# A gated decode step: the output product in 16 whole and 16 halved row groups, with TensorE's end in a third code block

## The chip, the cores and the metric

The kernel runs on one core of one Trainium2 chip. A time is the device time of one execution in microseconds. A core has five engines that run their own programs and meet at semaphores: TensorE (matmuls), VectorE, ScalarE, GpSimd, and SyncE, which here issues all transfers from memory.

## What is computed

Four sequences decode one token each. One branch is attention over the last 4096 positions of a key and value cache (32 query heads on 8 key/value heads), the other is a gated feed-forward layer on the same token; a scalar gate per sequence mixes them.

```python
W = min(4096, max(256, Sk // 4))                       # 4096
q = (x @ wq) -> [4, 32, 1, 128]
k, v = the last W positions of k_cache, v_cache, each kv head for 4 query heads
p = softmax(q @ k.T * 128 ** -0.5)
a = (p @ v) -> [4, 4096] @ wo                           # wo: 4096 x 512
gate, up = x @ W_gate, x @ W_up                        # 512 x 1792 each
b = (gate * (gate > 0) * up) @ W_down                  # 1792 x 512
g = sigmoid((x * gate_w).sum(-1, keepdims=True))
return g * a + (1 - g) * b
```

x is 4 x 1 x 512, all arrays are bf16.

## The kernel before

The caches are worked through in eight sets (`NSET`), each one sequence and four of its eight kv heads: 4 MB of keys and 4 MB of values. All loads go through SyncE's single queue in the order that `_dma_order` writes out: wq, x, the gate weights, then keys and values in turn, W_gate and W_up, the last values, W_down, and wo in pieces. Memory on the core has four big slots; the values of all sets use the same one, so the values of a set wait until the value product (PV) of the set before is done (`_slots`).

A set s goes through these steps, in the order that `_order` writes out. VectorE transposes the keys in four parts (EKT), TensorE multiplies each part with the queries (SC, eight matmuls), VectorE masks and takes maxima (ESC), a small matmul spreads the maximum (SW), ScalarE takes the exponential (EXP), VectorE transposes the probabilities (EPT), and TensorE multiplies them with the values (PV, 32 matmuls: 16 on the first half of the slot, 16 on the second). ScalarE, for the last set also VectorE, copies the result to `osb` (NORM).

After the last set's scores TensorE computes gate and up (GU) and the sums of the softmax (RS), then PV of the last set. RELU on ScalarE and H on VectorE make the hidden row, EHT transposes and gates it. OQ (8 matmuls) and EOQ arrange the attention output into `oq`; FFN (14 matmuls) multiplies the hidden row by W_down, and WO multiplies `oq` by wo, both into the same accumulator. FIN copies the result, half on ScalarE and half on VectorE, and SyncE sends it out.

WO has 32 row groups i of 128 rows each. A group is either one whole matmul of 512 columns, or two half products of 256 columns that go to different columns of the array and different output rows (0 to 3 and 64 to 67); FIN reads the one half of the result from the first rows and the other from the second. `WHOLE` says how many groups are whole. `WO_PIECES` cuts wo into pieces in units of half a group (64 units of 64 KB); each piece is one transfer with a semaphore of its own, and the first matmul of a piece waits for it.

TensorE's program is not unrolled over the sets. It is cut into blocks (setup, turn, gates, half, first, value, mix, tail) with branches between them, and the semaphores are counted down as they are taken (`E.take`) so that the same code serves each set. At its start it marks a place, `here`, and a branch at its end, whose condition is never true, is announced there with `branch_hint(here)`. The other engines' programs have such an announced branch at their ends too, and GpSimd, ScalarE and SyncE place theirs at an aligned address with `addr_align`.

## Time and profile before

| | |
|---|---|
| median of the runs shown | 195.67 us (195.67, 195.49, 196.94) |
| the profiled execution's own time | 197.35 us |
| its span, first to last instruction | 194.6 us |
| data moved | 81.01 MB, 416 GB/s over the span |
| mean granted TensorE clock | 0.877 of full speed |
| matmuls in WO | 27 of 512 columns, 10 of 256 columns |

The span is the time from the first to the last of the program's own instructions; the execution's own time has 2.75 us more around it. PE is TensorE's matmuls, PEld its weight loads, DVE VectorE, ACT ScalarE, POOL GpSimd, SP SyncE; a q behind a name is that engine's sequencer. In rows of the timeline the first number is the start, the second the duration, and brackets hold the idle time before and what ended it. In the table of windows each engine has its busy time with the number of instructions, then follow the granted clock, the share of the transfer engines and GB/s. In the table of transfers the last number is the median time from issue to landing.

### The profile page before, as it was taken

The numbers are of one execution on the slowest core, as the hardware profiler recorded it, in microseconds if no ns is written. First come the engines' busy times: TensorE is split into PE (matmuls) and PEld (weight loads), VectorE is DVE, ScalarE is ACT, GpSimd is POOL, SyncE is SP. The second block draws the span as 40 slices with busy tenths as digits, with TensorE's granted clock in tenths as the row PEclk, the third lists the DMA queues.
The fourth block names the chain that finished last, engine by engine and source line by source line (L and its number), as shares of the span: only waits on it lengthen the run. The fifth ranks groups of instructions, "written<-read, shape, count | busy, mean of one in ns | idle before, by whom it ended". The sixth has DMA issues, their size and how long they took to land. (4 is left out here: it accounts for less than half of the span.)

```text
span 194.6 us, 1787 instructions
## 1 busy us (share of the span) xinstructions
PE 122.3 (63%) x651; PEld 56.4 (29%) x651; DVE 126.1 (65%) x156; ACT 30.5 (16%) x51; POOL 18.8 (10%) x42
## 2 busy tenths in 40 slices
PE   0025078489576927692779285928692879645896
PEld 0011022135122402340234022402340234222584
DVE  5114779999699459935993599359935993280300
ACT  2000000042220340034003400340034003400100
POOL 5984000100100010001000100010001000100000
PEclk9999558999969985999589969985999589997999
DMA  6999999999999999999999999999999989999991
GB/s 216 431 439 431 431 438 431 438 445 445 408 421 445 431 431 438 431 445 431 431 431 431 431 438 438 431 431 431 431 431 445 431 377 427 435 424 424 418 417 76
DMA packets 3906, 81.01 MB, mean 416 GB/s; under 512 B 441, under 2 KB 450, under 8 KB 834
## 3 DMA queue, kind: packets, MB, share of 16 engines
q1 hardware_dynamic: 3906, 81.01, 97.4%
HBM read 81.01 MB, written 0.00 MB: 416 GB/s over the span
## 5 line engine op out<-in xcount | busy, mean ns | idle before, releaser
L342 PE MATMUL bank<-kt,qblk 128*128 128x512 bf16 x256 | 73.6, 447 | 30.4 <-PEq L84 30.4
L560 DVE STREAM_TRANSPOSE kt<-slots 128x2048 f32<-128x2048 f32 x32 | 73.0, 2299 | 5.4 <-DMA slots<-in_A_k_cache_dram 5.4
L342 PEld LDWEIGHTS bank<-kt,qblk 128*128 128x128 bf16 x256 | 26.8, 110 | 73.5 <-issue 56.1
L342 PE MATMUL bank<-slots,pT 128*64 128x512 bf16 x256 | 31.0, 395 | 15.5 <-PEq L84 15.5
L598 DVE CUSTOM_DVE_ANT_0 sc<-bank,maskf 128x512 bf16<-128x512 f32 x32 | 21.5, 670 | 26.5 <-PE bank L342 26.5
L342 PEld LDWEIGHTS bank<-slots,pT 128*64 128x64 bf16 x256 | 17.4, 113 | 28.4 <-issue 20.6
L674 ACT ACTIVATE osb<-bank 32x256 bf16<-32x256 f32 x30 | 11.3, 375 | 89.2 <-PE bank L342 89.0
L688 ACT ACTIVATE pe<-sc,negmax 128x2048 bf16<-128x2048 bf16 x8 | 16.0, 2002 | 46.2 <-DVE negmax L608 46.2
L613 DVE STREAM_TRANSPOSE pT<-pe 128x2048 bf16<-128x2048 bf16 x8 | 18.3, 2285 | 2.2 <-ACT pe L688 2.2
L329 POOL COPY qblk<-qblk 128x576 bf16<-128x576 bf16 x8 | 5.3, 668 | 144.4 <-PE bank L342 144.4
L346 PE MATMUL bank<-identb,xsb 5*128 5x5 bf16 x4 | 0.3, 173 | 13.1 <-DMA xsb<-in_A_x_dram 13.1
L342 PE MATMUL bank<-rd,grpb 128*128 128x32 bf16 x8 | 1.4, 176 | 9.5 <-PEq L84 9.5
L342 PE MATMUL bank<-slots,oq 128*68 128x512 bf16 (+1 forms) x37 | 6.6, 350 | 0.0
L651 DVE CAST xsb<-bank 4x256 bf16<-4x256 f32 x1 | 0.4, 418 | 8.9 <-PE bank L342 8.9
L342 PEld LDWEIGHTS bank<-slots,oq 128*68 128x68 bf16 (+1 forms) x37 | 5.6, 164 | 1.0 <-issue 0.3
L342 PE MATMUL bank<-slots,xT 128*8 128x512 bf16 (+1 forms) x64 | 5.2, 486 | 0.6 <-DVE negmax L608 0.4
L564 DVE COPY xT<-bank 128x16 bf16<-128x16 bf16 x1 | 0.2, 166 | 7.7 <-PE bank L346 7.7
L622 DVE CAST osb<-bank 32x256 bf16<-32x256 f32 x2 | 0.8, 424 | 6.6 <-PE bank L342 6.6
L342 PEld LDWEIGHTS bank<-rd,grpb 128*128 128x128 bf16 x8 | 0.8, 96 | 13.2 <-issue 13.2
L346 PEld LDWEIGHTS bank<-identb,xsb 5*128 5x128 bf16 x4 | 0.2, 114 | 13.1 <-DMA xsb<-in_A_x_dram 13.1
L318 POOL MEMSET oq<- 128x4096 bf16 x1 | 3.5, 3512 | 0.1
L297 POOL TENSOR_SCALAR_AFFINE_SELECT fold<-fold 128x256 bf16<-128x256 bf16 x8 | 3.3, 418 | 1.1
(51 smaller groups left out, 39.1 us busy)
## 6 DMA issues: line engine op xcount, KB each, us to landing
slots<-in_A_k_cache_dram SPq DMA_DIRECT2D x8, 4096.0 KB, 24.8
slots<-in_A_v_cache_dram SPq DMA_DIRECT2D x6, 4096.0 KB, 15.6
slots<-in_A_v_cache_dram SPq DMA_DIRECT2D x4, 2048.0 KB, 12.6
slots<-in_A_wq_dram SPq DMA_DIRECT2D x1, 4096.0 KB, 12.3
slots<-in_B_W_gate_dram SPq DMA_DIRECT2D x1, 1792.0 KB, 19.3
slots<-in_B_W_up_dram SPq DMA_DIRECT2D x1, 1792.0 KB, 23.0
slots<-in_B_W_down_dram SPq DMA_DIRECT2D x1, 1792.0 KB, 17.6
slots<-in_A_wo_dram SPq DMA_DIRECT2D x1, 1408.0 KB, 19.7
```

Source lines behind the costliest of these rows:

```text
L297: op(lambda: e.affine_select(dst, src, pattern, cmp, fill, base=base, channel_multiplier=mult), ev)
L318: op(lambda: e.memset(oq[:, :, :], 0.0), ("PADQ",))
L329: E.op(lambda s=s: e.tensor_copy(qblk[:, 0, :, :, :], qblk[:, (s + 1) % NSET, :, :, :]), ev=("QC", s), ctr="qc", waits=[("SC", s, 3)])
L342: E.op(lambda: t.matmul(out_, lhsT, rhs, start=start, stop=stop, tile_position=pos, skip_group_check=True), ev=ev, waits=waits)
L346: E.op(lambda: t.transpose(out_, in_, idn), ev=ev, waits=waits)
L560: E.op(lambda: v.transpose(kt[:, f % 2, :].bitcast(FP32), slot("k", s)[:, 4096 * f:4096 * f + 4096].bitcast(FP32)), ev=("E", "KT", s, f), ...
L598: E.op(lambda: v.tensor_tensor_reduce(sc[:, 512 * f:512 * f + 512], banks[scb(key)], R["maskf"][:, :], 1.0, -3.0e38, ALU.add, ALU.max, mx4 ...
L613: E.op(lambda: v.transpose(pT[:, :], pe[:, :]), ev=("E", "PT", s), ctr="pt", waits=[("EXP", s)] + ([("PV", s - 1)] if s else []) + ([("V", ...
L622: norm(E, lambda d, p: v.tensor_copy(d, p), s, ((0, 1), (1, 1)), "NORMV")
L651: E.op(lambda: v.tensor_copy(osum[:, 256:512], banks[ACX][64:68, 256:512]), ev=("OSUM", 1), waits=[("WO", "P")])
L674: norm(E, lambda d, p: a.activation(d, p, ACTF.Copy), s, parts[0:2 if s == NSET - 1 else 4], "NORM")
L688: E.op(lambda: a.activation(pe[:, :], sc[:, :], ACTF.Exp, bias=negmax[:, s % 2:s % 2 + 1], scale=SCALE, accum_out=rowsum[:, s:s + 1]), ev= ...
```

## The change

`WHOLE` goes from 27 to 16, and wo comes in four pieces instead of five. The first half of the last values waits for the first half of the product of set 6 (`PVH`) instead of all of it; the second half waits for all of it. VectorE does the last EPT behind H instead of ahead of it. In TensorE's program the branch out of `mix` becomes the one that is announced at the program's start; in `tail` a second place is marked, and the never-taken branch at the end is announced there. It now stands in a block of its own, `leave`, behind a jump that is aligned to 256 instructions with an offset of 4.

```diff
-WHOLE = 27
-WO_PIECES = ((0, 22), (22, 38), (38, 50), (50, 60), (60, 64))
+WHOLE = 16
+WO_PIECES = ((0, 30), (30, 50), (50, 60), (60, 64))
...
                 elif it == ("v", NSET - 1):
-                    load(("V", "a"), "d_v", slot(*it)[:, 0:8192], src[:, :, 0:8192], waits=w)
-                    load(("V", "b"), "d_vb", slot(*it)[:, 8192:16384], src[:, :, 8192:16384])
+                    load(("V", "a"), "d_v", slot(*it)[:, 0:8192], src[:, :, 0:8192], waits=[("PVH", NSET - 2)])
+                    load(("V", "b"), "d_vb", slot(*it)[:, 8192:16384], src[:, :, 8192:16384], waits=w)
...
             run("OQ", "FFN")
             for p in range(len(WO_PIECES) - 1):
                 WO(p)
-            t.br("pe_tail")
+            t.br_lt(at, 0, on_true="pe_mix", on_false="pe_tail").branch_hint(here)
         with block("tail"):
+            here = t.mark_branch_hint_location()
             WO(len(WO_PIECES) - 1)
+            t.addr_align(256, offset=4, max_nops=0)
+            t.br("pe_leave")
+        with block("leave"):
             t.br_lt(at, 0, on_true="pe_tail", on_false="pe_end").branch_hint(here)
...
         elif k == "GU":
             act.append(("RELU",))
-            dve += [("H",), ("EHT",)]
+            dve += [("H",), ("EPT", NSET - 1), ("EHT",)]
         elif k == "PT":
-            dve.append(("EPT", it[1]))
+            dve += [("EPT", it[1])] * (it[1] < NSET - 1)
```

## The prediction

> **What bounds the kernel now.** I read the page's head first, then the chain that ended last, then the timeline of the last 30 us with the transfer table beside it.

> ```profile
> span 194.6 us, 1787 instructions
> PE 122.3 (63%) x651; PEld 56.4 (29%) x651; DVE 126.1 (65%) x156; ACT 30.5 (16%) x51; POOL 18.8 (10%) x42
> DMA  6999999999999999999999999999999989999991
> q1 hardware_dynamic: 3906, 81.01, 97.4%
> ```

> No compute engine is busy more than 65%, while the one data queue holds the 16 transfer engines for 97.4% of the span. The body of the kernel is a stream of 81 MB; only the first and the last slices are not full. A change to TensorE or VectorE in the middle moves nothing; what can move is how soon the kernel ends after the last byte. The chain shows that end:

> ```profile
> 177.44 3.56 PE bank L342 x16
> 181.03 0.04 DVE osb L622
> 181.46 0.44 DVE osb L622
> 181.95 10.78 PE bank L342 x59
> 192.76 0.42 DVE xsb L651
> ```

> From 177.44 on it is TensorE alone: the second half of the last value product (16 matmuls), the copies, and then 59 matmuls in a row: 8 of OQ, 14 of FFN, 37 of WO. Now the transfers that feed them (issue times in the first block, median time to landing in the second, the five output-weight issues in the last line):

> ```profile
> 144.53 0.43 SPq L242 DMA_DIRECT2D slots<-in_B_W_up_dram  x1
> 162.75 1.20 SPq L242 DMA_DIRECT2D slots<-in_A_v_cache_dram  x2
> 163.99 0.59 SPq L242 DMA_DIRECT2D slots<-in_B_W_down_dram  x1
> ...
> slots<-in_B_W_up_dram SPq DMA_DIRECT2D x1, 1792.0 KB, 23.0
> slots<-in_B_W_down_dram SPq DMA_DIRECT2D x1, 1792.0 KB, 17.6
> slots<-in_A_wo_dram SPq DMA_DIRECT2D x1, 1408.0 KB, 19.7
> slots<-in_A_wo_dram SPq DMA_DIRECT2D x1, 1024.0 KB, 21.8
> slots<-in_A_wo_dram SPq DMA_DIRECT2D x1, 768.0 KB, 23.2
> slots<-in_A_wo_dram SPq DMA_DIRECT2D x1, 640.0 KB, 24.3
> slots<-in_A_wo_dram SPq DMA_DIRECT2D x1, 256.0 KB, 24.4
> ...
> L242 SPq DMA_DIRECT2D slots<-in_A_wo_dram x5: 334/432/433, 165.3 to 167.1; - x5
> ```

> Issue plus landing: W_down is there at 163.99 + 17.6 = 181.6; the five pieces of wo, issued about 0.45 apart, at 185.0, 187.6, 189.4, 191.0 and 167.1 + 24.4 = 191.5. So the last byte is there at 191.5, and that is the floor under everything that this change does.

> ```profile
> 182.94 3.30 PE L342 MATMUL bank<-slots,hg 128*68 128x512 bf16 x14
> 186.08 6.63 PE L342 MATMUL bank<-slots,oq 128*68 128x512 bf16 x37
> 192.00 0.42 PEld L342 LDWEIGHTS bank<-slots,oq 128*4 128x4 bf16 x10 [0.33 <-issue]
> 193.23 0.29 SPq L242 DMA_DIRECT2D out_dram<-xsb  x1
> ```

> The output product ends at 186.08 + 6.63 = 192.71, 1.2 after the last byte. TensorE, not the transfer, ends last, but by little.

> **The change, part by part.**

> *Half products for whole ones.* Of the 37 matmuls of WO, 27 are whole (512 columns) and 10 are halves; afterwards it is 16 and 32, 48 in all.

> ```profile
> L342 PE MATMUL bank<-slots,oq 128*68 128x512 bf16 x27 | 6.0, 379 | 0.0
> L342 PE MATMUL bank<-slots,oq 128*4 128x256 bf16 x10 | 0.7, 273 | 0.0
> ```

> A whole group takes (192.00 - 186.08) / 27 = 0.219. Of the halves, the last ends at 192.71 and lasts 0.273, so the five pairs start from 192.00 to 192.44: four steps, 0.11 a pair. The two halves of a pair lie in different columns of the array and run side by side. Eleven row groups turned from 0.219 into 0.11 save 1.2 us of TensorE time.

> *Four output pieces.* The borders 30, 50, 60, 64 replace 22, 38, 50, 60, 64. From 185.0 to 191.5 the queue moved 42 of the 64 units, 0.155 each, so the new first piece, eight units larger, lands at 185.0 + 8 x 0.155 = 186.2; 50, 60 and 64 stay at 189.4, 191.0 and 191.5. One issue of 0.43 us leaves SP's queue; it was issued 20 us ahead of its need, so it is worth nothing.

> *The new end.* The first 15 groups, all whole, cannot start before 186.2 + 0.1 and take 3.3, to 189.6. The second piece has one whole group and nine pairs, 1.2, to 190.8. The third is there at 191.0 and has five pairs, 0.55, to 191.65. The last two pairs start then, at 191.65 and 191.76, and the last matmul ends at 191.76 + 0.27 = 192.03 instead of 192.71. That is 0.68 off the span; all that follows (copy, output transfer) is unchanged.

> *An earlier wait for the first half of the last V.* It now waits for the first half of PV 6 rather than all of it and is issued some 2 us before 162.75. What it queues behind, W_up, lands only at 144.53 + 23.0 = 167.5, 4.8 after the old issue. The transfer engines had work in hand, so nothing lands earlier: 0. The second half keeps the old wait, W_down and wo stand behind it on SP and are issued about 0.6 earlier, with the same result. Without that 4.8 us of backlog the step would have been worth up to 2 us.

> *EPT 7 behind H.*

> ```profile
> 169.97 2.31 DVE L613 STREAM_TRANSPOSE pT<-pe 128x2048 bf16<-128x2048 bf16 x1 [2.16 <-ACT pe L688]
> 170.03 0.54 ACT L682 ACTIVATE sc<-bank 128x448 bf16<-128x448 f32 x1
> 172.20 0.92 DVE L638 TENSOR_TENSOR sc<-sc,bank 128x448 bf16<-128x448 bf16 x1
> 172.57 1.92 PE L342 MATMUL bank<-slots,pT 128*64 128x512 bf16 x16 [2.31 <-PEq L84]
> 177.44 3.55 PE L342 MATMUL bank<-slots,pT 128*64 128x512 bf16 x16 [2.95 <-PEq L84]
> ```

> H needs RELU, done at 170.57, and takes 0.92; the transpose then runs from 171.5 to 173.8, and the first half of PV 7 starts at 174.1 instead of 172.57. It has to be done by 177.44, when the second half gets its data: 3.3 us are left for what took 1.92. What it does to the clock is read in windows of 3.41 us, laid on the steps of the granted clock:

> ```profile
> 150.07:153.48 3.41, 1.77 (x5) 0.68 (x6) 3.41 (x2) 0.43 (x2) 0.00 (x0) 0.50 1.05 452
> 153.48:156.89 3.41, 3.41 (x10) 1.15 (x9) 3.41 (x5) 0.00 (x0) 0.00 (x0) 0.50 0.98 423
> 156.89:160.31 3.42, 2.22 (x17) 1.10 (x17) 3.42 (x4) 0.00 (x0) 0.00 (x0) 1.00 0.85 362
> 170.55:173.96 3.41, 1.39 (x14) 0.96 (x16) 3.34 (x4) 0.02 (x1) 0.00 (x0) 1.00 1.03 437
> 173.96:177.37 3.41, 0.53 (x6) 0.05 (x2) 0.48 (x3) 0.00 (x0) 0.00 (x0) 1.00 0.98 416
> 177.37:180.79 3.42, 3.35 (x16) 1.48 (x16) 0.00 (x0) 0.00 (x0) 0.00 (x0) 0.50 0.99 422
> 180.79:184.20 3.41, 2.46 (x16) 1.98 (x15) 1.68 (x4) 0.75 (x2) 0.00 (x0) 1.00 0.99 415
> ```

> The first number is TensorE's busy time, the third from the end its clock. The clock of a window follows the work of the one before: 0.53 of 3.41 busy was followed by 0.50, 1.39 by 1.00; from 0.50, 1.77 was too little to rise and 3.41 enough. With the product moved, the window from 170.55 is empty, the first half runs at 0.50 from 174.1 to 177.6 and fills its window, and the second half then runs at 1.00: 1.9 instead of 3.55, ending near 179.5. Of these 1.5 us nothing reaches the end: FFN can start 1.2 earlier, when W_down lands, but the output product waits for 186.2 either way. If the windows lie otherwise and both halves run cold, the second ends near 181.1 as now, FFN ends at 186.2, and the end is the same. The wait at 186.2 is not long enough to lose the clock: at most 1.5 of 3.41 idle, and 1.39 busy sufficed. Taken at 0, with 0.2 of loss as its other bound.

> [...] Eleven more matmuls with their weight loads, a hint and a jump make the program longer, and the end is placed in a block of its own. For the cost of going there I have these rows:

> ```profile
> L498 PEldq COMPARE_BRANCH  x8: 73/217/217, 44.8 to 177.5; - x8
> L507 PEldq COMPARE_BRANCH  x1: 73/73/73, 191.6 to 191.6; - x1
> ```

> A taken branch took 217 ns and one that falls through 73. Lower bound: 0.3 for hint and jump. Upper bound: the block comes from memory when the jump asks for it. The nearest row is the output transfer, 1.4 us from its issue at 193.23 to the end of the span at 194.6; with 16 KB through one of 16 engines at the stream's 431 GB/s (27 each, 0.6), some 2.0 us, an estimate. Both lie beside other work: the jump stands behind the last matmul, is reached near 191.7, and the copies and the output transfer cover it until 194.6 - 0.7 = 193.9. So I take 0 inside the span. What is not covered is what TensorE does after its last instruction, which no row here shows: 0 to two such loads, 4.0 us, or as much gained.

> [...]

> **Sum.** The profiled execution took 197.35 us for a span of 194.6, with 2.75 around it. Less 0.7, it would take 196.65 with a span of 193.9. It is the slow one: the runs shown have a median of 195.67. If in those the second half of PV 7 already ran at 1.00, the old kernel's FFN ended near 184.8 and its output product kept up with its pieces (two whole groups and three pairs after 191.0 + 0.1, 0.76; then two pairs, ending 191.97 + 0.27 = 192.24), and the gain is only 192.24 - 192.03 = 0.2. Between 0.2 and 0.7 I take 0.45: **195.2 us**.

> **The rivals.**

> *It does nothing* (195.7): the last byte at 191.5 sets the end anyway, if the old kernel mostly keeps up. For it: only 1.2 us between byte and product; against it: 0.7 of them is plain to see. Chance 0.07.

> *Code comes late* (slower). [...] One load of 2.0 gives 197.2, still within 1%; two give 199.2. It decides once more than 2.4 us lie bare. [...] Chances 0.05 and 0.13.

> *The code behind the end gets shorter* (faster): if part of the 2.75 us around the span is such a load already and the new layout hides it, 195.2 - 2.0 = 193.2. Nothing in the page shows that it is. Chance 0.06.

> **How the numbers follow.** The forecast has 0.69. A measurement of this kernel tells about 1% from no change (its three runs span 0.7%). Faster by over 1%: 0.06. Slower: 0.13. Within: 0.69 + 0.07 + 0.05 = 0.81. The range leaves out the two far cases, 0.19: from 194.2 (the 0.7 of gain and half the runs' scatter) to 197.2 (one load).

> **What would show it.** Right: 16 whole and 32 half matmuls at 0.22 and 0.11; the second half of PV 7 at 1.00; the last matmul ending within 0.6 of the last landing; a span near 193.9. Wrong: a span that ends with TensorE's branch instead of the output's landing; a time around the span that differs from 2.75 by more than 1; output groups at 0.50.

## The result and the profile after

| | before | after |
|---|---|---|
| median | 195.54 us (195.33 to 197.01, 20 runs) | 196.67 us (196.23 to 198.07, 20 runs) |
| ratio, 95% interval | | 1.0049 (1.0031 to 1.0066) |
| span of the profiled execution | 194.6 us | 195.0 us |
| first copy of the result begins, us | 192.76 | 191.75 |
| output transfer issued, us | 193.23 | 192.22 |

The change makes the kernel 0.5% slower; the forecast was 195.2 us, 0.2% faster. In the profiled executions the work that computes the result ends a whole microsecond earlier and the program ends 0.4 us later. The ratios here and below lie nearer to those of the means than of the medians, and the few runs over 1.5% above the fastest of their kernel are left out of them, but not out of the medians and ranges.

The rows below are, in this order, from the head and the queues of the page after, from its chain, and from the timeline of its last 22 us.

```profile
span 195.0 us, 1811 instructions
q1 hardware_dynamic: 3762, 81.01, 97.1%
q8 instruction: 1, 0.02, 0.0%
...
165.09 20.87 DMA slots<-in_A_wo_dram
186.01 5.71 PE bank L342 x48
191.75 0.42 DVE xsb L655
...
173.85 6.57 PE L342 MATMUL bank<-slots,pT 128*64 128x512 bf16 x32 [3.80 <-PEq L84]
181.38 1.06 PE L342 MATMUL bank<-osb,fold 128*64 128x256 bf16 x8 [0.95 <-DVE osb L626]
182.37 3.30 PE L342 MATMUL bank<-slots,hg 128*68 128x512 bf16 x14
186.01 5.70 PE L342 MATMUL bank<-slots,oq 128*68 128x512 bf16 x48 [0.34 <-DMA slots<-in_A_wo_dram]
191.32 0.10 PEld L342 LDWEIGHTS bank<-slots,oq 128*4 128x4 bf16 x4 [0.20 <-DMA slots<-in_A_wo_dram]
192.22 0.29 SPq L242 DMA_DIRECT2D out_dram<-xsb  x1
```

In the chain the transfer of wo now stands ahead of the output product, 20.87 us from the first issue to the first landing, and then come 48 output matmuls that end at 186.01 + 5.71 = 191.72. The last of them start when the last piece lands, 191.32. That is the output product as intended. The new line in the head is the other: a queue "instruction" with one packet of 0.02 MB, which the page of before does not have. Two more views show whose it is. The first is the source view of TensorE's last three branches and of its second announcement, L506 (count, shortest, median and longest in ns, then when), the second the transfers between 192.2 and 193.6.

```profile
L504 PEldq COMPARE_BRANCH  x1: 73/73/73, 190.7 to 190.7; - x1
L506 PEldq BRANCH_PREFETCH_HINT  x1: 31/31/31, 190.9 to 190.9; - x1
L508 PEldq COMPARE_BRANCH  x1: 3535/3535/3535, 191.3 to 191.3; - x1
L511 PEldq COMPARE_BRANCH  x1: 85/85/85, 194.9 to 194.9; - x1
...
q8 instruction: 1, 0.02, 5.6%
```

L508 is the aligned jump into `leave`, the "third code block" of the title. The "third" is my own count of the program, which no run shows; what the profile shows is that the jump takes 3535 ns, from 191.3 to 194.86, and that one block of 16 KB (16384 bytes in the trace) is loaded meanwhile by the instruction queue (5.6% of 16 engines' 1.4 us is 1.25 us on one engine). Only then come the last branch, L511, and the end of the span. The output transfer, issued at 192.22, is over 1.4 us later as before, at 193.6. So the bare part of the jump is 195.0 - 193.6 = 1.4 us: it eats the 1.0 that the output product had gained and 0.4 more.

The profiled execution of before had 2.75 us around its span, that of after 2.2. Both executions are among the longest of their kernel. The medians over runs say more: before, span 194.3 and 1.3 around it (35 runs beside the first experiments); after, 195.0 and 1.6 (20 runs). So about two thirds of the loss is in the span and the rest around it.

### The profile page after: what moved, and what is told of

It is laid out like the page before. It is cut to its first block, busy times and chain, and to the rows that moved or that the text cites. A ratio compares the mean times of both kernels' runs of the same rounds, so it can differ in the third digit from the quotient of the medians.

```text
span 195.0 us, 1811 instructions
## 1 busy us (share of the span) xinstructions
PE 124.6 (64%) x662; PEld 55.8 (29%) x662; DVE 125.8 (65%) x156; ACT 30.4 (16%) x51; POOL 18.7 (10%) x42
## 2 busy tenths in 40 slices
DMA  6999999999999999999999999999999989999991
## 3 DMA queue, kind: packets, MB, share of 16 engines
q1 hardware_dynamic: 3762, 81.01, 97.1%
HBM read 81.01 MB, written 0.00 MB: 415 GB/s over the span
## 5 line engine op out<-in xcount | busy, mean ns | idle before, releaser
L342 PE MATMUL bank<-kt,qblk 128*128 128x512 bf16 x256 | 75.3, 456 | 29.7 <-PEq L84 29.7
L342 PEld LDWEIGHTS bank<-kt,qblk 128*128 128x128 bf16 x256 | 27.3, 112 | 74.1 <-issue 57.3
L342 PE MATMUL bank<-slots,pT 128*64 128x512 bf16 x256 | 32.1, 407 | 12.2 <-PEq L84 12.2
L342 PEld LDWEIGHTS bank<-slots,pT 128*64 128x64 bf16 x256 | 17.4, 116 | 26.5 <-issue 18.7
L342 PE MATMUL bank<-rd,grpb 128*128 128x32 bf16 x8 | 1.4, 176 | 9.5 <-PEq L84 9.5
L342 PE MATMUL bank<-slots,oq 128*4 128x256 bf16 (+1 forms) x48 | 5.7, 311 | 0.3 <-DMA slots<-in_A_wo_dram 0.3
L342 PE MATMUL bank<-slots,xT 128*8 128x512 bf16 (+1 forms) x64 | 5.3, 489 | 0.6 <-DVE negmax L612 0.4
L342 PEld LDWEIGHTS bank<-slots,oq 128*4 128x4 bf16 (+1 forms) x48 | 4.2, 122 | 1.9 <-DMA slots<-in_A_wo_dram 1.1
L342 PEld LDWEIGHTS bank<-rd,grpb 128*128 128x128 bf16 x8 | 0.8, 96 | 13.2 <-issue 13.2
## 6 DMA issues: line engine op xcount, KB each, us to landing
slots<-in_B_W_gate_dram SPq DMA_DIRECT2D x1, 1792.0 KB, 19.3
slots<-in_B_W_up_dram SPq DMA_DIRECT2D x1, 1792.0 KB, 23.0
slots<-in_B_W_down_dram SPq DMA_DIRECT2D x1, 1792.0 KB, 18.3
```

Source lines behind the costliest of these rows:

```text
L342: E.op(lambda: t.matmul(out_, lhsT, rhs, start=start, stop=stop, tile_position=pos, skip_group_check=True), ev=ev, waits=waits)
```

## The experiments

Each ran 12 times beside the kernel before on the same chip, in three groups. The median of before was 195.66 us in the first (the end alone, all but the end, the early jump, the announced jump), 195.87 in the second (half products alone, order alone, the late announcement, no announcement) and 195.76 in the third (one announcement, all halves).

**The end alone, and everything but the end.** The first kernel is before with nothing but the new end:

```diff
             for p in range(len(WO_PIECES) - 1):
                 WO(p)
-            t.br("pe_tail")
+            t.br_lt(at, 0, on_true="pe_mix", on_false="pe_tail").branch_hint(here)
         with block("tail"):
+            here = t.mark_branch_hint_location()
             WO(len(WO_PIECES) - 1)
+            t.addr_align(256, offset=4, max_nops=0)
+            t.br("pe_leave")
+        with block("leave"):
             t.br_lt(at, 0, on_true="pe_tail", on_false="pe_end").branch_hint(here)
```

> The kernel before with the new end alone (both announced branches and the aligned jump; 27 whole groups, five pieces, all else as before). Theory, the jump is the loss: the jump behind the last matmul is issued near 192.2 and takes 3.5 us again, so TensorE ends near 195.8, 1.2 behind the output transfer, and the time is 1.2 to 2 us above before (196.7 to 197.6). Rival, the new matmuls or the order on VectorE cost the time: no change, 195.5.

The second is after with those lines taken back to what before has:

> The changed kernel with the end as before (no jump, no second announcement; 16 whole groups, four pieces, both order changes kept). Theory, the jump is the whole loss: the span ends with the output transfer, near 193.6, and the time is 0.5 to 1.0 below before (194.5 to 195.0). [...]

| | median (range) | ratio (95%) | span |
|---|---|---|---|
| the end alone | 196.67 (196.08 to 197.78) | 1.0046 (1.0020 to 1.0072) | 194.6 |
| all but the end | 194.99 (194.82 to 196.41) | 0.9949 (0.9917 to 0.9980) | 193.8 |

From the first, the jump in the source view and the head; from the second, the head, the chain, the last branch and the output transfer:

```profile
L508 PEldq COMPARE_BRANCH  x1: 2963/2963/2963, 191.5 to 191.5; - x1
span 194.6 us, 1790 instructions
```

```profile
span 193.8 us, 1808 instructions
...
165.28 20.89 DMA slots<-in_A_wo_dram
186.21 5.71 PE bank L342 x48
191.94 0.42 DVE xsb L651
...
L507 PEldq COMPARE_BRANCH  x1: 73/73/73, 191.5 to 191.5; - x1
...
192.41 0.29 SPq L242 DMA_DIRECT2D out_dram<-xsb  x1
```

The end by itself makes before as slow as after. In the profiled execution its jump sticks out by 0.5 us and not by the 1.2 that I expected, since it is reached at 191.5 and not at 192.2 and takes 2963 ns. But this execution is the shortest of the twelve; over the runs the median span is 195.05 against 194.3 of before. The end costs 1.0 on before (196.67 against 195.66) and 1.7 on all but the end (after's 196.67 against 194.99). Without it the span ends with the output transfer (192.41 + 1.4), the last branch takes 73 ns, and no instruction load is listed in the span. This version is faster than both kernels, and it is the best of the study.

**Half products alone, order alone.** Two more versions split what is left. One is all but the end, with the V waits and the EPT order of before; the other is all but the end with the output product of before:

```diff
# half products alone
-load(("V", "a"), ..., waits=[("PVH", NSET - 2)])
-load(("V", "b"), ..., waits=w)
+load(("V", "a"), ..., waits=w)
+load(("V", "b"), ...)
-dve += [("H",), ("EPT", NSET - 1), ("EHT",)]
+dve += [("H",), ("EHT",)]
-dve += [("EPT", it[1])] * (it[1] < NSET - 1)
+dve.append(("EPT", it[1]))
# order alone
-WHOLE = 16
-WO_PIECES = ((0, 30), (30, 50), (50, 60), (60, 64))
+WHOLE = 27
+WO_PIECES = ((0, 22), (22, 38), (38, 50), (50, 60), (60, 64))
```

> The kernel before with 16 whole groups and four pieces alone; the end, the wait of the last values and the order on VectorE as before. Theory, the half products are the whole gain of the run with the old end and all other edits (194.99): again 194.9 to 195.1, the last matmul within 0.6 of the last landing. Rival, the later EPT and the clock that it keeps bring the gain: about 195.5.

> The kernel before with the two order changes alone (earlier wait of the last values, EPT behind H); 27 whole groups, five pieces, the end as before. Theory: what they free ahead of FFN is eaten by 27 whole groups; at most 0.2 to 0.4 below before (195.3 to 195.6). Rival, they bring the gain of the run with the old end: 195.0.

| | median (range) | ratio (95%) | span |
|---|---|---|---|
| half products alone | 195.52 (194.88 to 198.04) | 0.9975 (0.9943 to 1.0007) | 193.8 |
| order alone | 195.43 (195.22 to 195.93) | 0.9964 (0.9938 to 0.9989) | 194.7 |

Output product in the chain of the first, then of the second:

```profile
186.29 5.71 PE bank L342 x48
```

```profile
185.55 5.92 PE bank L342 x25
191.48 1.37 PE bank L342 x12
192.88 0.42 DVE xsb L651
```

Half products alone end at 192.00, the old product at 192.85. Half a microsecond of that is not the product's: the second profile is of the longest of its twelve executions, and its last piece of wo landed at 192.06 instead of 191.54 (read from the trace's single semaphore updates and packets, called the records below). Counted from the last landing, the products end 0.46 and 0.79 later; the end alone, which has the old product too, has 0.80.

Six of the first one's twelve times lie at 194.88 to 195.09, as all but the end; the others lie at 195.94 or above, so its median says little and the interval includes no change. I read the half products as worth 0.3 to 0.45 (0.3 counted from the landing, 0.45 between the lowest times, 194.88 against 195.32). The lowest times of the order alone, 195.22 to 195.32, are within 0.1 of before's lowest. Its interval excludes no change all the same, because its times end at 195.93 and 16 of the 35 of before lie above that. So the order lowers the floor by 0.1 at most; whether it makes the longer executions rarer, one set of twelve does not settle. The sum of the two, 0.4 to 0.55, fits all but the end against before: 0.5 between the lowest times (194.82 against 195.31) and 195.66 - 194.99 = 0.67 between medians.

**Can the load be brought forward?** If the jump's price is a late load, an earlier load should hide it. The first try keeps the old end and puts the aligned jump ahead of `mix`, well before the end:

```diff
-            t.br_lt(at, NSET, on_true="pe_half", on_false="pe_mix")
+            t.br_lt(at, NSET, on_true="pe_half", on_false="pe_over")
+        with block("over"):
+            t.addr_align(256, offset=4, max_nops=0)
+            t.br("pe_mix")
```

> The changed kernel with the aligned jump moved from behind the last matmul to ahead of OQ, where TensorE's matmuls of the last value product run for 3 us; one announced branch at the end as before. Theory: the jump takes 3.5 us from 177.3 to 180.8 and OQ can start at 181.4 as it did, so the span is near 193.6 and the time 0.5 to 1.0 below before (194.5 to 195.0). [...]

196.54 us (196.14 to 200.05), ratio 1.0030 (0.9991 to 1.0069), span 195.0. The jump in the source view, the transfers between 48.7 and 49.9, the issue of the values of the third set, and the output product; the last line is that same issue in all but the end:

```profile
L500 PEldq COMPARE_BRANCH  x1: 186/186/186, 178.9 to 178.9; - x1
...
q8 instruction: 1, 0.02, 5.5%
...
66.85 0.54 SPq L242 DMA_DIRECT2D slots<-in_A_v_cache_dram  x1
...
187.49 5.66 PE L342 MATMUL bank<-slots,oq 128*68 128x512 bf16 x48 [1.23 <-DMA slots<-in_A_wo_dram]
...
65.57 0.54 SPq L242 DMA_DIRECT2D slots<-in_A_v_cache_dram  x1
```

The jump itself is now nearly free, 186 ns. The time stayed above 195.5 all the same: 16 KB were loaded near 49 us, 130 us ahead, and that was not free. The issue of values comes at 66.85 instead of 65.57, 1.28 later, and the output product begins 187.49 - 186.21 = 1.28 later too. The load took 1.06 us (5.5% of 16 engines' 1.2) of one transfer engine while the data queue held the sixteen for 97.2% of the span, and a later transfer, spread over all sixteen, waits for that one. The records show it: of the sixteen parts of the first piece of wo fifteen land by 186.10 and the last at 187.45, where in all but the end all sixteen land by 186.17.

The second try announces the jump: at the start of `mix` a place is marked, a taken branch at the end of `tail` is announced there, and the aligned jump is kept only as a filler that is never run:

```diff
         with block("mix"):
+            there = t.mark_branch_hint_location()
             run("OQ", "FFN")
...
         with block("tail"):
-            here = t.mark_branch_hint_location()
             WO(len(WO_PIECES) - 1)
+            t.br_lt(at, NSET + 1, on_true="pe_leave", on_false="pe_pad").branch_hint(there)
+        with block("pad"):
             t.addr_align(256, offset=4, max_nops=0)
             t.br("pe_leave")
         with block("leave"):
-            t.br_lt(at, 0, on_true="pe_tail", on_false="pe_end").branch_hint(here)
+            t.br_lt(at, 0, on_true="pe_tail", on_false="pe_end")
```

> The changed kernel with the way into the third block made a taken branch that is itself announced, at the start of the block ahead of OQ. Theory, the load starts only when the branch is reached because what is announced is the branch behind it: now the branch takes under 0.5 us instead of 3.5, the span is near 193.6 and the time 0.5 to 1.0 below before. Rival, an announcement loads nothing ahead: 3.5 us as in the changed kernel, 196.5.

197.71 us (196.14 to 198.09), ratio 1.0065 (1.0032 to 1.0099), span 196.4. The branch, the transfers between 185.0 and 186.3, the chain, and two windows of the output product (TensorE's busy time first, its clock third from the end):

```profile
L508 PEldq COMPARE_BRANCH  x1: 373/373/373, 193.2 to 193.2; - x1
...
q8 instruction: 1, 0.02, 5.1%
...
165.13 22.15 DMA slots<-in_A_wo_dram
187.32 7.28 PE bank L342 x48
194.62 0.42 DVE xsb L657
...
183.90:187.30 3.40, 1.04 (x5) 0.59 (x3) 0.00 (x0) 0.00 (x0) 0.00 (x0) 1.00 0.98 408
187.30:190.60 3.30, 3.28 (x11) 2.16 (x12) 0.00 (x0) 0.00 (x0) 0.00 (x0) 0.69 0.96 392
```

The announcement is issued at 177.5, and the branch takes 373 ns instead of 3535: this announcement did bring the block ahead of need (the load at 185.1, the branch at 193.2). What the load waits for after the announcement is not shown. It again falls into the stream, and the first piece of wo takes 22.15 us to land instead of 20.87. TensorE then idles long enough to lose its clock (laid on the clock's own steps, 1.23 busy of 3.41 from 185.14, then 0.50 from 188.55), and runs the output product at a mean of 0.69 in the next window: 7.28 us instead of 5.71. Five of the twelve runs lie at 196.14 to 196.41 and seven at 197.69 to 198.09; the profiled one is of the long kind. That the short kind is the late stream without the lost clock fits its 1.2 over all but the end, but no run of that kind was profiled.

The third try announces the same branch late, at the start of `tail`, when the stream has nearly ended; all else is as in the second:

```diff
         with block("mix"):
-            there = t.mark_branch_hint_location()
             run("OQ", "FFN")
...
         with block("tail"):
+            there = t.mark_branch_hint_location()
             WO(len(WO_PIECES) - 1)
             t.br_lt(at, NSET + 1, on_true="pe_leave", on_false="pe_pad").branch_hint(there)
```

> The changed kernel with the taken branch into the third block announced at the start of the tail, as late as the second announcement stood. Theory: the load starts near 191.3 instead of 192.3, after the stream, and TensorE ends near 193.9 instead of 194.9, under the cover of the output transfer: 195.1 to 195.6. Rival, the announcement is too late or starts a load in the last pieces of the stream: 196.0 to 197.0.

196.65 us (196.38 to 197.16), ratio 1.0034 (1.0011 to 1.0058), span 195.5.

```profile
L508 PEldq COMPARE_BRANCH  x1: 3806/3806/3806, 191.6 to 191.6; - x1
```

Announced 0.4 us ahead, the branch waits in full; which lead between 0.4 and 15.7 us would do, no run here shows. The fourth run takes only the second announcement out of after, to see whether it does anything there:

```diff
         with block("tail"):
-            here = t.mark_branch_hint_location()
             WO(len(WO_PIECES) - 1)
...
         with block("leave"):
-            t.br_lt(at, 0, on_true="pe_tail", on_false="pe_end").branch_hint(here)
+            t.br_lt(at, 0, on_true="pe_tail", on_false="pe_end")
```

> The changed kernel without its second announcement (no mark in the tail, the last branch unannounced); the jump stays. Theory: the second announcement does nothing for the jump, which again takes 3 to 3.8 us, 196.4 to 196.8. Rival, it shortens the load: the jump takes longer, or the load falls into the stream, 197.5 or more.

196.89 us (195.99 to 197.43), ratio 1.0040 (1.0013 to 1.0067), span 195.7.

```profile
L507 PEldq COMPARE_BRANCH  x1: 3623/3623/3623, 192.0 to 192.0; - x1
```

The jump waits as long as in after; the second announcement changes nothing that can be measured.

**What keeps the old end free of a load?** All but the end, with the announcement taken off its last branch:

```diff
-        here = t.mark_branch_hint_location()
...
-            t.br_lt(at, 0, on_true="pe_tail", on_false="pe_end").branch_hint(here)
+            t.br_lt(at, 0, on_true="pe_tail", on_false="pe_end")
```

> The changed kernel with the old end, and its one announcement taken away (the never-taken branch stays, the mark at the start goes). [...] Rival, the announcement does nothing: 195.0, no load in the span.

196.22 us (196.05 to 198.63), ratio 1.0027 (0.9993 to 1.0060), span 194.9. Its transfers between 174.5 and 175.7, and its chain:

```profile
q8 instruction: 1, 0.02, 5.6%
...
187.35 5.68 PE bank L342 x48
```

I had put it at 196.0 to 196.5, with a load in the stream. Without the announcement a 16 KB block is loaded at 174.6 us, and the output product begins 1.14 later than in all but the end (187.35 against 186.21). Which block it is, the record does not name. Of the sixteen parts of the first piece of wo two are late here: one lands at 186.92, 0.75 behind the last of all but the end, and in each transfer since about 81 us, where no load is listed, a part was about that late; the other lands at 187.31, 1.14 behind, and that lateness begins at the load. The product begins 1.14 later and not 1.89, so the two do not add, and the later one sets the loss. The announced branch that is never taken thus keeps this load from happening; the edit shows that, and not how the loader decides.

**How long the program may get without a load.** If half products are good, are all halves better? `WHOLE = 0` on all but the end adds 16 matmuls and 16 weight loads. I expected 194.9 to 195.2 as in all but the end, or 196.0 and more if a load fell into the span.

```diff
-WHOLE = 16
+WHOLE = 0
```

> The run with the old end and all other edits, with all 32 groups as half products: 16 more matmuls, 32 more instructions, no jump. [...]

197.32 us (196.63 to 199.58), ratio 1.0085 (1.0045 to 1.0125), span 195.5. The head, the transfers between 47.5 and 48.7, the same issue of values as above, and the end of the chain:

```profile
span 195.5 us, 1840 instructions
...
q8 instruction: 1, 0.02, 5.5%
...
66.81 0.54 SPq L242 DMA_DIRECT2D slots<-in_A_v_cache_dram  x1
...
192.11 0.71 PE bank L342 x10
192.82 0.46 issue
193.29 0.40 PE bank L342 x4
```

The lower forecast did not hold. A load stands near 48 us, as with the jump ahead of `mix`, and the values are issued at 66.81, 1.24 behind 65.57. With 16 whole groups (1808 instructions in the head) the span has no such load, and 32 instructions later (1840) it has one; what brings it, and where the border lies, no run shows. Another half microsecond is lost at the end: by the records the last piece landed at 192.70, and its matmuls start only at 193.29, where all but the end starts them 0.04 after the landing (191.47 and 191.51). The chain calls this gap issue, and its cause stays open.

## Why the prediction was wrong, and where it was right

**The step that failed** is the jump into `leave`, the term that the prediction took at 0 inside the span. It priced the jump at up to 2.0 us, put it near 191.7 and let the copies and the output transfer cover it until 193.9. The jump was reached at 191.3, the cover ended at 193.6, and the jump took 3.5 us (3.0 to 3.8 in four kernels). So the cover was 2.3, about as sized, and 1.4 us lay bare in the span, 1.3 of the jump and 0.1 of the branch behind it. The load was sized from two pieces, 1.4 for a transfer's latency and 0.6 for its bytes. The records of after show three: the load starts 0.96 us after the jump is issued, takes 1.27 on one engine, and TensorE goes on 1.3 after that. The way in and back took 2.3 and not 1.4, and the bytes twice the 0.6. No row of the page before shows the 16 KB that the 2.0 us of a load, and with it the top of the range, were reckoned from; the trace of after shows a load of 16384 bytes. The prediction named the sign to look for, a span that ends with TensorE's branch, and that is what the profile shows.

The measured 196.67 lies inside the stated range only because the range ran up to the rival of one bare load, 197.2; the forecast itself pointed the other way. That rival is the nearest in kind, but it put its load behind the end of the program, and most of the loss came on the way into the block. That two blocks would be loaded behind the end, its far case of 199.2, no run shows: the traces of before and after hold one such load each there, at 196.4 and 196.5 us.

**A second term was misread**: the 2.75 us around the span. The sum took it as given and bought rivals from it, the code that is loaded behind the end. It belongs to one long execution; over the runs before has 1.3 in the median. The records of before's profiled execution have a 16 KB instruction load behind the span, at 196.4 us; so have those of after, and of three experiments whose time around the span is 1.6 to 2.3. Such a load is thus not new with the change. Yet the four kernels whose jump waits for its block have 1.5 to 1.6 around the span in the median, and the other experiments and before have 1.2 to 1.4. This last third of the loss goes with the jump, and what it consists of stays open.

**Right, with its size.** The output product: forecast to start at 186.2 and end at 192.03, measured 186.01 and 191.72, with whole groups and pairs at 0.22 and 0.11. The last matmul ended 0.45 after the last landing (191.27 to 191.72 by the records, and in all but the end 191.47 to 191.92), within the 0.6 given. For an old product that keeps up with its pieces the forecast had an end of 192.24, and in the end alone it ended there; to the digit that is luck, since the last landing was 191.44 and not 191.5. The gain without the jump was forecast at 0.2 to 0.7, taken as 0.45; all but the end measured 0.67 between medians and 0.5 between the lowest times. The earlier V wait was costed at nothing, and together with the EPT order it lowered the floor by no more than 0.1. The four pieces, costed at nothing too, were run only together with the half products.

**Wrong in its detail, right in its price:** EPT 7 behind H. The product began at 173.85 (forecast 174.1), but its second half did not run at full clock. From the windows of after, laid as those of before:

```profile
169.58:172.99 3.41, 0.28 (x2) 0.19 (x2) 2.61 (x2) 0.67 (x3) 0.00 (x0) 1.00 1.05 447
172.99:176.40 3.41, 2.55 (x13) 1.26 (x15) 1.70 (x5) 0.00 (x0) 0.00 (x0) 0.50 0.97 414
176.40:179.82 3.42, 3.42 (x19) 1.49 (x17) 0.00 (x0) 0.00 (x0) 0.00 (x0) 0.50 1.02 432
179.82:183.23 3.41, 2.46 (x18) 1.73 (x15) 1.59 (x4) 0.75 (x2) 0.00 (x0) 1.00 1.03 436
```

The windows lay otherwise than I had put them: the product's start, 173.85, is 0.86 inside a window, and 2.55 busy of 3.41 was not enough to rise from 0.50. The product ended at 180.4 instead of 179.5. As forecast this did not matter, since FFN was over at 185.67 and the output product waited for 186.01.

## What to carry to other kernels

Code that has to be loaded during the kernel cost something either way here: a wait of 3.0 to 3.8 us if the block was asked for by the jump, or 1.1 to 1.3 us of a saturated stream if it was fetched ahead. So after a tail is made longer, look for an instruction queue in the profile; the best version here keeps the gain and has no such load in its span. What covers a wait on a path that ends the kernel must be measured against the whole of such a wait, its start and its return included, not against the bytes moved.
